# Routing split into eight planned steps with its temporaries in PSUM, a longer planned transpose, and a new table of order

## The chip, the core and the metric

The kernel runs on one core of one Trainium2 chip. The metric is device time in microseconds (us). The core has a matrix engine (PE), a vector engine (DVE), an activation engine (ACT), a general engine (POOL) and a queue engine that issues transfers (SP). Each takes its own instructions strictly in the order in which they were written, and engines wait for each other at semaphores.

## What is computed

Three stages in a row, on 1,536 tokens of 512 numbers: attention with a window of 128 and 4 sink positions, a dense layer of 2,048 hidden units with a rational activation, and a mixture of 8 experts in which each token goes to the expert of its largest logit and only as many tokens per expert as a capacity allows are kept.

```python
scores = scale * np.matmul(q, k.transpose(0, 1, 3, 2))
scores = np.where(is_sink | in_window, scores, -1000000000.0)
a = softmax(scores); x = np.matmul(a, v)
h = x @ w_in
g = (a[0] + a[1]*h + a[2]*h**2 + a[3]*h**3) / (1 + abs(b[0])*abs(h) + abs(b[1])*h**2 + 1e-6)
x = g @ w_out
logits = x @ w_gate
expert_idx = np.argmax(logits, axis=1)
gate_w = softmax(logits)[np.arange(N), expert_idx]
...
for i in range(N):          # in order of tokens
    e = expert_idx[i]
    if counts[e] < capacity:
        disp[e, counts[e]] = x[i]; pos[i] = counts[e]; counts[e] += 1; keep[i] = True
h = np.maximum(np.einsum('ecd,edf->ecf', disp, w1), 0.0)
y = np.einsum('ecf,efd->ecd', h, w2)
out[i] = gate_w[i] * y[expert_idx[i], pos[i]]       # for kept i
```

## The kernel before

All large products are made of half-precision pairs (a high and a low part), three matmuls for one. The work comes in these kinds.

- **Attention halves** (`half(n)`, 24 of them): scores (L649), mask, maximum and exponentials, transposes by PE (L707, L711), the product with v (L763, L765), and the split of the result into the tile `xt`.
- **Conversion of weights** (`conv`): each piece of w_in and w_out arrives as 64-bit numbers and is turned into a high and a low half. A letter per piece, in the strings CI and CO, says how: P and R use PE matmuls (L285 opens a bank, L279 subtracts), S and G finish on POOL (L335, L355), V finishes on DVE (L345). S and R keep a temporary `wf` in SBUF.
- **Units** (`unit(U)`, 24): four groups of 12 matmuls each (L827) of the dense layer for 256 tokens, then the rational function (`rat1` on ACT and DVE, `rat2` on POOL, `sig` on ACT), ended on DVE by L1433 from a bank or by L862 from SBUF, as the string RE says, and for the first two groups of tokens split into halves (`split`, L363 and then L366 on POOL or L369 on DVE, as the string GS says).
- **Gate columns** (`wg_group(f)`, 16): once piece f of w_out is converted, two transposing transfers (L877) bring it into a buffer `wf`, of which there are three, and 12 small matmuls (L885) multiply it with the gate's weights.
- **Bursts** (`burst`) add the units' shares of the logits; `logits` brings them to the layout by tokens (L971, L974).
- **Routing** of the first 512 tokens: `route` chooses the largest logit (`choose`, `first_max`: L955 to L981), counts the tokens per expert before each (`places`: L988, L990, the two matmuls L992 and L993, then L995 to L997) and works out the gate (`gates`, L1002 to L1006). `pick` then takes the expert with the most tokens (L1032 to L1051).
- **The chosen expert**: `ffn_y` multiplies the first 384 tokens with w_out (L1106) as soon as `pick` is through; the expert's own weights then take w_out's place; `hid` (L1126) and `outp` (L1150) follow. Remaining tokens' units go on meanwhile, and `count_rest` at the end says whether anything is left for a loop that isn't entered with these inputs.

The order of instructions on all engines is set before the program exists, by a planner (`Plan`). Each step is a generator that yields what it needs, an engine, a planned time and buffers, such as `yield DVE(1.9, "b")` for 1.9 us of DVE and a bank, and then writes its instructions. The planner takes the step that can start first on its engine, and among equal ones that with the smallest key. `DVL` is a DVE step that may not run beside POOL in the plan; `lat=` is added to the planned end of an SP step before a follower may start. Keys, and which engine does what, come from the table PRM. Where the plan leaves PE idle before 150 us and a bank is free, `idle` writes small filler matmuls (L490) that compute nothing, so that the matrix engine doesn't rest.

In `route`, all of `choose` and `places`, PE's two matmuls among them, are one step that is planned as 1.9 us of DVE:

```python
bs = slice(0, FB)
yield DVE(1.9, "b")
kb = plan.got("b")
mx = choose(bs)
places(bs, bank(kb))
plan.give("b", kb)
yield ACT(0.6)
gates(bs, mx)
```

So the two matmuls are written into PE's order at the point that PE's plan has reached by then, and take no planned time there.

Of the kernel before, what the change touches and what calls it, by code (L numbers as in the profile page):

```python
# [8 lines left out]
F32 = mybir.dt.float32  # L9
# [10 lines left out]
P = 128  # L20
# [8 lines left out]
E = 8  # L29
# [6 lines left out]
CH = 256  # L36
NCH = NT // CH
NU = 4 * NCH
PRM = dict(LA=11.877, RATE=1.2, LC=6.882, LO=2.195, BATCH=1, T0=-13.679, dS=1.29, TW=53.523, dW=7.072,
           T1=-22.973, d1=6.206, T2=67.305, d2=5.26, CI='PSPPSGGGGGGGVPPG', CO='GGGSVGPRVSSSSGPP',  # L40
           RE='PPPPSPPPPPSPPSSSPPPPPPSS', CC='G', LL=3, rb=5, gp=5, GS='GGGGGGGG', VE=1, rr=19.539, rs=36.318,
           rt=-29.499, LD=-6.009, TF=150, FG=0.033, NE=7, eps=0, WT=-60.39, NB=4, VS1=14, BK=-29.251, dK=12.297,
           dO=0.252, eb=2, SE='G', st=2, wf=3, rc=1, xt=2, ab=2, qb=2)


class Plan:
# [147 lines left out]
def SP(dur, *take, lat=0.0):  # L194
    return "SP", dur, take, lat, None, None
# [10 lines left out]
def _build(ctx, tc, nc, io, ns, window, cap):  # L206
# [36 lines left out]
    def bank(k):  # L243
        return (bps[0] if k < R["NB"] else bps[1]).tile([P, 512], F32, name=f"b{k}")
# [704 lines left out]
    keep = gat.tile([P, NBLK], F32, name="keep")  # L949
    run = gat.tile([P, NBLK + 1, E], F16, name="run")  # L950

    def first_max(dst, src, n):

        mx = sm.tile([P, NBLK], F32, name="fm")[:, :n]
        V.tensor_reduce(out=mx, in_=src, axis=AX.X, op=ALU.max)  # L955
        iv = sm.tile([P, NBLK, E], F32, name="fi")[:, :n]
        V.tensor_tensor(out=iv, in0=src, in1=mx.unsqueeze(2).to_broadcast([P, n, E]), op=ALU.is_ge)
        V.tensor_tensor(out=iv, in0=iv, in1=iom.unsqueeze(1).to_broadcast([P, n, E]), op=ALU.mult)
        ix = sm.tile([P, NBLK], F32, name="fx")[:, :n]
        V.tensor_reduce(out=ix, in_=iv, axis=AX.X, op=ALU.min)  # L960
# [13 lines left out]
        V.tensor_copy(out=lg[:, b0:b0 + nb, :], in_=lt[:, 0:nb * E].rearrange("p (t e) -> p t e", e=E))  # L974
        plan.give("b", kb)

    def choose(bs):

        n = bs.stop - bs.start
        mx, _ = first_max(oh[:, bs, :], lg[:, bs, :], n)  # L980
        V.tensor_copy(out=oh16[:, bs, :], in_=oh[:, bs, :])  # L981
        return mx

    def places(bs, pt):

        n = bs.stop - bs.start
# [34 lines left out]
    NSB = NST // P
# [6 lines left out]
    def pick():  # L1028
# [594 lines left out]
```

## Time and profile before

| | us |
|---|---|
| median of 3 runs (lowest, highest) | 341.65 (340.46, 343.74) |
| time of the profiled execution | 342.39 |
| its span, first instruction to last | 340.8 |
| PE busy, share of the span | 321.9, 94% |
| DVE busy | 258.8, 76% |
| ACT busy | 236.6, 69% |
| POOL busy | 199.7, 59% |
| mean granted clock of PE | 0.986 |

Busy time of PE counts the filler matmuls too. [...]

### The profile page before, as it was taken

To read this page: it belongs to the slowest core of one execution; us is meant where nothing else is said; L and a number is where in the kernel's file an instruction comes from. 1 tells how busy PE (TensorE), PEld (TensorE's weight loads), DVE (VectorE), ACT (ScalarE), POOL (GpSimd) and SP (SyncE) were. 2 spreads that over 40 slices of the span, in tenths; PEclk is the share of its full clock that TensorE was granted. 3 is DMA by queue.
4 is the path that set the end of the run, shared out by engine and by line. 5 is a ranking of instruction groups with operands and counts; after the bars stand their busy time and mean duration, and the time that the engine had idled before them with its cause. 6 is when DMAs were issued, how large, how long until landed. Compare 5 with 4: busy or idle time off the path is not lost.

```text
span 340.8 us, 9053 instructions
## 1 busy us (share of the span) xinstructions
PE 321.9 (94%) x3586; PEld 237.7 (70%) x3586; DVE 258.8 (76%) x505; ACT 236.6 (69%) x587; POOL 199.7 (59%) x211
## 2 busy tenths in 40 slices
PE   8999999989999889999999969999999999999991
PEld 5666787767878767878867748556676688787540
DVE  4988799899899898999898967502248689786541
ACT  2798989987989889897889746304255678686600
POOL 5466869759989587889998735305001156465400
PEclk9999999999999999999999969999999999999998
DMA  7655764727869998454861203000005320000011
GB/s 231 232 196 179 243 214 138 262 78 237 191 168 228 268 171 315 116 146 146 206 141 27 87 9 124 2 1 2 2 0 191 133 111 0 2 2 0 15 50 38
DMA packets 32744, 41.79 MB, mean 123 GB/s; under 512 B 19832, under 2 KB 19832, under 8 KB 32696
## 3 DMA queue, kind: packets, MB, share of 16 engines
q1 hardware_dynamic: 32696, 41.15, 41.6%
q8 instruction: 30, 0.49, 0.6%
q14 instruction: 18, 0.15, 0.2%
HBM read 30.66 MB, written 6.29 MB: 108 GB/s over the span
## 4 chain that ended last, share of the span: by engine, by line
PE 75%; DVE 14%; ACT 4%; DMA 3%; issue 2%; DVEq 0%; ACTq 0%
PE b L827 29%; PE b L1106 9%; PE b L490 7%; PE b L1150 5%; PE b L1126 5%; PE b L765 4%; PE sc L649 4%; PE b L707 3%; PE b L922 3%; DMA wf<-wout 2%; DVE b L315 2%; DVE g L1433 1%; PE b L279 1%; DMA st<-w_out 1%; PE b L763 1%
## 5 line engine op out<-in xcount | busy, mean ns | idle before, releaser
L827 PE MATMUL b<-xt,win 128*128 128x256 f16 x1152 | 139.6, 276 | 0.3
L827 PEld LDWEIGHTS <-win 128*128 128x128 f16 x1152 | 112.1, 100 | 21.1 <-issue 5.7
L852 POOL TENSOR_TENSOR rb<-rb,rc 128x1024 f32<-128x1024 f32 x24 | 57.5, 2396 | 1.4
L699 POOL TENSOR_TENSOR e<-e,rs 128x512 f32<-128x512 f32 x24 | 24.9, 1039 | 37.6 <-DVE rs L686 26.7
L831 ACT ACTIVATE rb<-b 128x512 f32<-128x512 f32 x48 | 28.9, 604 | 19.3 <-PE b L827 17.2
L835 DVE TENSOR_TENSOR g<-g,b 128x512 f32<-128x512 f32 x48 | 32.6, 681 | 10.8 <-ACT g L833 10.6
L849 POOL TENSOR_SCALAR rc<-rb,cof 128x1024 f32<-128x1024 f32 x24 | 28.9, 1202 | 20.0 <-ACT rb L831 19.7
L833 ACT ACTIVATE g<-b,cof 128x512 f32<-128x512 f32 x48 | 37.5, 784 | 0.0
L837 DVE SCALAR_TENSOR_TENSOR g<-g,cof,b 128x512 f32<-128x512 f32 x48 | 35.5, 742 | 0.7
L734 POOL TENSOR_SCALAR_AFFINE_SELECT upp<-low 128x512 f32<-128x512 f32 x20 | 13.4, 671 | 36.6 <-ACT low L728 36.5
L679 ACT ACTIVATE e<-sc,nm 128x132 f32<-128x132 f32 x84 | 31.3, 372 | 1.9
L1106 PE MATMUL b<-gs,wout 128*128 128x384 f16 x192 | 32.6, 326 | 0.0
L490 PE MATMUL b<-const-bfloat16-1.0 128*1 128x256 bf16 x201 | 29.5, 291 | 1.8 <-PEq L1612 0.9
L855 ACT ACTIVATE rb<-rb 128x1024 f32<-128x1024 f32 x24 | 25.6, 1065 | 3.7 <-POOL rb L852 3.7
L1106 PEld LDWEIGHTS <-wout 128*128 128x128 f16 x192 | 18.4, 99 | 13.2 <-issue 1.8
L490 PEld LDWEIGHTS <-const-bfloat16-1.0 128*1 128x1 bf16 x201 | 16.0, 88 | 12.4 <-issue 6.2
L1433 DVE SCALAR_TENSOR_TENSOR g<-g,cof,b 128x512 f32<-128x512 f32 x34 | 24.3, 742 | 0.5
L649 PE MATMUL sc<-kt,qt 64*64 64x128 f32 (+4 forms) x672 | 19.8, 249 | 1.9 <-DVE rs L682 1.9
L649 PEld LDWEIGHTS sc<-kt,qt 64*64 64x64 f32 x672 | 17.0, 132 | 6.0 <-issue 2.1
L1421 ACT ACTIVATE b<-rb 128x512 f32<-128x512 f32 x34 | 20.3, 611 | 0.5 <-DVE wgo L896 0.4
L366 POOL TENSOR_TENSOR gs<-g,gs 128x1024 f16<-128x1024 f32 (+1 forms) x8 | 13.2, 1649 | 10.5 <-ACT gs L363 10.5
L1108 ACT ACTIVATE gse<-b 128x384 f16<-128x384 f32 x4 | 2.0, 491 | 24.9 <-PE b L1106 24.9
(183 smaller groups left out, 626.8 us busy)
## 6 DMA issues: line engine op xcount, KB each, us to landing
st<-w_in SPq DMA_DIRECT2D x16, 512.0 KB, 4.1
st<-w_out SPq DMA_DIRECT2D x16, 512.0 KB, 3.9
st<-w SPq DMA_DIRECT2D x8, 512.0 KB, 3.3
kt<-k SPq DMA_DIRECT2D x12, 264.0 KB, 4.2
qt<-q SPq DMA_DIRECT2D x12, 256.0 KB, 3.6
v<-v SPq DMA_DIRECT2D x12, 256.0 KB, 2.9
xs<-xt SPq DMA_DIRECT2D x12, 256.0 KB, 3.3
out<-wf SPq DMA_DIRECT2D x12, 256.0 KB, 4.7
```

Source lines behind the costliest of these rows:

```text
L490: T.matmul(out=fp[0:1, 0:256], lhsT=one[:, 0:1], rhs=one, start=True, stop=True)
L649: T.matmul(out=out, lhsT=q[:, t], rhs=kk[:, a:z], start=True, stop=True)
L679: A.activation(out=e[:, h, :], in_=wv[:, h, :], func=AF.Exp, scale=0.125, bias=nm[:, h:h + 1], accum_out=su[:, h:h + 1])
L827: T.matmul(out=out, lhsT=l, rhs=r, start=(j == 0), stop=(j == len(jobs) - 1))
L831: A.activation(out=bb, in_=hp, func=AF.Abs, scale=2.0 ** -16)
L833: A.activation(out=g, in_=hp, func=AF.Identity, scale=cof[:, 3:4], bias=cof[:, 2:3])
L835: V.tensor_tensor(out=g, in0=g, in1=hp, op=ALU.mult)
L837: V.scalar_tensor_tensor(out=g, in0=g, scalar=cof[:, 1:2], in1=hp, op0=ALU.add, op1=ALU.mult)
L849: (G if eng == "G" else V).tensor_scalar(out=cc, in0=bb, scalar1=cof[:, 5:6], scalar2=cof[:, 4:5], op0=ALU.mult, op1=ALU.add)
L852: G.tensor_tensor(out=bb, in0=bb, in1=cc, op=ALU.mult)
L1106: T.matmul(out=yp[:, :n], lhsT=l, rhs=r, start=(j == 0), stop=(j == len(jobs) - 1))
L1433: V.scalar_tensor_tensor(out=g, in0=g, scalar=cof[:, 0:1], in1=rp[U, z], op0=ALU.add, op1=ALU.mult)
```

## The change

The step of the routing is cut into eight: choose (1.2 us of DVE planned), counts (0.8, DVL), places (0.2 of PE, now a PE step of its own), kept, gates_in, gates_exp, gates_out. The temporaries of `first_max`, `places`, `gates` and `pick`, tiles in SBUF before, lie in unused columns of the PSUM bank that the step holds anyway; `count_rest` takes a bank for it. What stays in SBUF are `lg`, `oh`, `oh16`, `run`, `keep`, `gw`. `pick` becomes two DVE steps and holds its bank longer. The transposes of `wg_group` are planned as 1.3 us with 2.2 us behind them (1.2 and 1.2 before). PRM gets other numbers throughout, and so every engine another order. Of the 24 units, 13 end by P instead of 17 (RE), two splits move from POOL to DVE (GS), and of the 32 pieces of weights (CI and CO together) 5 instead of 8 go by P, 3 instead of 1 by R, 3 instead of 7 by S, 16 instead of 13 by G and 5 instead of 3 by V.

```diff
-           T1=-22.973, d1=6.206, T2=67.305, d2=5.26, CI='PSPPSGGGGGGGVPPG', CO='GGGSVGPRVSSSSGPP',
-           RE='PPPPSPPPPPSPPSSSPPPPPPSS', CC='G', LL=3, rb=5, gp=5, GS='GGGGGGGG', VE=1, rr=19.539, rs=36.318,
+           T1=-23.716, d1=7.69, T2=79.004, d2=7.972, CI='PRGGGGGGGGGGRPPG', CO='GGVVVVPRVSSSGGGP',
+           RE='PPPPSPPPPPSPSPSSSSSPPSSS', CC='G', LL=3, rb=5, gp=5, GS='GGGGVVGG', VE=1, rr=50.47, rs=75.665,
...
-        yield SP(1.2, "wf", lat=1.2)
+        yield SP(1.3, "wf", lat=2.2)
...
-    def first_max(dst, src, n):
-
-        mx = sm.tile([P, NBLK], F32, name="fm")[:, :n]
+    def first_max(dst, src, n, pb):
+
+        mx, ix, iv = pb[:, 0:n], pb[:, 32:32 + n], in_bank(pb, n)
         V.tensor_reduce(out=mx, in_=src, axis=AX.X, op=ALU.max)
-        iv = sm.tile([P, NBLK, E], F32, name="fi")[:, :n]
...
+    def in_bank(pb, n):
+        return pb[:, 64:64 + n * E].rearrange("p (t e) -> p t e", e=E)
...
+    def counts(bs):
+
         if bs.start == 0:
             V.memset(run[:, 0, :], 0.0)
         for t in range(bs.start, bs.stop):
             V.tensor_tensor(out=run[:, t + 1, :], in0=run[:, t, :], in1=oh16[:, t, :], op=ALU.add)
...
     def route():
         bs = slice(0, FB)
-        yield DVE(1.9, "b")
+        yield DVE(1.2, "b")
         kb = plan.got("b")
-        mx = choose(bs)
-        places(bs, bank(kb))
+        pt = bank(kb)
+        pb = pt[:, NBLK * E:]
+        mx = choose(bs, pb)
+        yield DVL(0.8)
+        counts(bs)
+        yield PE(0.2)
+        places(bs, pt)
+        yield DVE(0.6)
+        kept(bs, pt, pb)
+        yield DVE(0.2)
+        gates_in(bs, mx, pb)
+        yield ACT(0.2)
+        gates_exp(bs, pb)
+        yield DVE(0.6)
+        gates_out(bs, pb)
         plan.give("b", kb)
-        yield ACT(0.6)
-        gates(bs, mx)
```

Three places of the new order. In these rows `b` with a number is a bank, `oh` the chosen expert of a token, `run` the counts, `wf` the buffer of the gate columns; line numbers are those of the version shown.

DVE at the routing, before:

```order
L974 COPY lg<-b_3609 128x32
L720 SCALAR_TENSOR_TENSOR sh_3593<-b_3591,sh_3593 32x128
L955 TENSOR_REDUCE fm<-lg 128x4
L957 TENSOR_TENSOR fi<-lg,fm 128x32
L958 TENSOR_TENSOR fi<-fi,iom 128x32
L960 TENSOR_REDUCE fx<-fi 128x4
L961 TENSOR_TENSOR oh<-fx,iom 128x32
L981 CAST oh_134<-oh 128x32
L988 MEMSET run 128x4
L990 TENSOR_TENSOR run<-run,oh_134 128x8 x4
L995 TENSOR_TENSOR po<-b_3649,oh 128x32
L996 TENSOR_REDUCE keep<-po 128x4
```

DVE at the routing, with the change:

```order
L972 COPY lg<-b_3646 128x32
L955 TENSOR_REDUCE b_3662<-lg 128x4
L956 TENSOR_TENSOR b_3662<-lg,b_3662 128x32
L957 TENSOR_TENSOR b_3662<-b_3662,iom 128x32
L958 TENSOR_REDUCE b_3662<-b_3662 128x4
L959 TENSOR_TENSOR oh<-b_3662,iom 128x32
L982 CAST oh_134<-oh 128x32
L835 TENSOR_TENSOR g_3532<-g_3532,b_3615 128x512
L988 MEMSET run 128x4
L990 TENSOR_TENSOR run<-run,oh_134 128x8 x4
L720 SCALAR_TENSOR_TENSOR sh_3659<-b_3657,sh_3659 32x128
L1465 SCALAR_TENSOR_TENSOR g_3265<-g_3265,cof,b_3712 128x512
```

The bank b_3662 stands where fm, fi and fx stood, and one step of a unit (L835) and a later pair of others now stand between the routing's own instructions; the first reader of the matmuls' result (L995 before) comes two rows below the end of this piece.

PE from the logits on, before, and the rows around the two matmuls of `places`:

```order
L971 MATMUL b_3609<-gsel,lacc_2592 128x8 x4
L279 LDWEIGHTS n_88
L279 MATMUL b_3572<-xt_3086,n_88 128x256
L827 LDWEIGHTS win_97
L827 MATMUL b_3622<-xt_2276,win_97 128x256
```

```order
L827 LDWEIGHTS win_98
L827 MATMUL b_3622<-xt_2276,win_98 128x256
L992 LDWEIGHTS tri_89
L992 MATMUL b_3649<-oh_134,tri_89 128x32
L993 LDWEIGHTS ones_86
L993 MATMUL b_3649<-run,ones_86 128x32
```

PE with the change, at the same two points:

```order
L969 MATMUL b_3646<-gsel,lacc_2445 128x8 x4
L707 MATMUL b_3652<-ident,e_3512 128x128 x4
L711 MATMUL b_3657<-ident,es_127 96x128
L649 MATMUL sc<-kt_2834,qt_3074 64x132
L649 MATMUL sc<-kt_3149,qt_3074 64x2x64
L649 MATMUL sc<-kt_3149,qt_3074 64x64
L649 MATMUL sc<-kt_2834,qt_3074 64x68
L649 MATMUL sc<-kt_2834,qt_3074 64x132
```

```order
L827 LDWEIGHTS win_98
L827 MATMUL b_3689<-xt_2309,win_98 128x256
L994 LDWEIGHTS tri_89
L994 MATMUL b_3662<-oh_134,tri_89 128x32
L995 LDWEIGHTS ones_86
L995 MATMUL b_3662<-run,ones_86 128x32
```

Between the logits' matmuls and those of `places` stand one subtraction and 12 matmuls of a unit before; with the change it is five transposes, 16 score matmuls and 24 matmuls of units.

SP at the first transposes, before:

```order
L295 DMA st_1595<-w_out 128x1024
L596 DMA v_1627<-v 128x512
L295 DMA st_1643<-w_out 128x1024
L877 DMA_TRANSPOSE wf_1701<-wout_99 128x4x128
L877 DMA_TRANSPOSE wf_1701<-wout_100 128x4x128
L295 DMA st_1728<-w_out 128x1024
L877 DMA_TRANSPOSE wf_1806<-wout_99 128x4x128
L877 DMA_TRANSPOSE wf_1806<-wout_100 128x4x128
L295 DMA st_1842<-w_out 128x1024
L877 DMA_TRANSPOSE wf_1876<-wout_99 128x4x128
L877 DMA_TRANSPOSE wf_1876<-wout_100 128x4x128
```

SP at the first transposes, with the change:

```order
L596 DMA v_1660<-v 128x512
L295 DMA st_1713<-w_out 128x1024
L877 DMA_TRANSPOSE wf_1742<-wout_99 128x4x128
L877 DMA_TRANSPOSE wf_1742<-wout_100 128x4x128
L877 DMA_TRANSPOSE wf_1765<-wout_99 128x4x128
L877 DMA_TRANSPOSE wf_1765<-wout_100 128x4x128
L877 DMA_TRANSPOSE wf_1797<-wout_99 128x4x128
L877 DMA_TRANSPOSE wf_1797<-wout_100 128x4x128
L295 DMA st_1833<-w_out 128x1024
```

Three pairs of transposes now follow each other with no other transfer between, where each pair had the load of a piece of w_out behind it.

Counted over the whole order, filler matmuls (L490) go from 201 to 164, L285 from 18 to 16 and L279 of 512 columns from 9 to 8; all other matmuls are the same in number. On DVE, the L369 of 512 elements go from 0 to 4, L345 from 3 to 5, L862 from 7 to 11, L1433 from 34 to 26; L325 into `wf` from 7 to 3. On POOL, L335 goes from 7 to 3, L355 from 20 to 19 and the splits of 512 elements (L366) from 8 to 4. Ahead of the logits of the first 512 tokens, PE has 720 matmuls of units where it had 672, and DVE 29 of L835 and of L837 where it had 28, and three L862 where it had two.

## Rows read from the trace of the kernel before

**Rows 1.** The page's first part: busy us of each engine, share, instructions

```profile
PE 321.9 (94%) x3586; PEld 237.7 (70%) x3586; DVE 258.8 (76%) x505; ACT 236.6 (69%) x587; POOL 199.7 (59%) x211
```

**Rows 2.** Sums by stretch: length, busy of each engine, clock, DMA share, GB/s

```profile
42.66:192.97 150.31, 144.15 (x1920) 114.67 (x1919) 139.35 (x261) 131.38 (x345) 123.23 (x114) 1.00 0.65 173
192.97:198.79 5.82, 2.70 (x27) 2.30 (x24) 4.90 (x15) 4.19 (x15) 4.71 (x4) 0.92 0.39 132
198.79:205.48 6.69, 6.69 (x37) 4.88 (x37) 2.83 (x12) 2.44 (x4) 1.26 (x2) 0.56 0.01 2
205.48:333.60 128.12, 128.12 (x1074) 87.70 (x1071) 77.29 (x136) 67.41 (x119) 44.09 (x30) 1.00 0.12 42
```

**Rows 3.** Timeline of PE around the routing: start, length, what, idle before it

```profile
193.99 1.47 PE L827 MATMUL b<-xt,win 128*128 128x256 f16 x12
198.15 0.19 PE L992 MATMUL b<-oh,tri 128*128 128x32 f16 x1 [2.69 <-DVE run L988]
198.77 0.19 PE L993 MATMUL b<-run,ones 128*128 128x32 f16 x1 [0.43 <-DVE run L990]
```

**Rows 4.** Timeline of DVE and POOL at the routing

```profile
194.06 0.19 DVE L974 COPY lg<-b 128x32 f32<-128x32 f32 x1 [0.54 <-PE b L971]
...
194.82 0.19 DVE L957 TENSOR_TENSOR fi<-lg,fm 128x32 f32<-128x32 f32 x1
...
195.05 0.53 DVE L958 TENSOR_TENSOR fi<-fi,iom 128x32 f32<-128x32 f32 x1
...
195.51 2.33 POOL L852 TENSOR_TENSOR rb<-rb,rc 128x1024 f32<-128x1024 f32 x1
...
195.83 2.06 DVE L961 TENSOR_TENSOR oh<-fx,iom 128x32 f32<-128x32 f32 x1
...
198.16 0.75 DVE L990 TENSOR_TENSOR run<-run,oh 128x8 f16<-128x8 f16 x4
...
198.99 0.19 DVE L995 TENSOR_TENSOR po<-b,oh 128x32 f32<-128x32 f32 x1
```

**Rows 5.** The chain that ended last: start, length, what

```profile
79.93 1.75 PE b L490 x15
...
114.52 3.93 PE b L827 x36
...
198.96 6.79 PE b L827 x36
...
208.65 2.64 PE b L827 x24
```

**Rows 6.** Groups by form: count, busy us, mean ns of one

```profile
L490 PE MATMUL b<-const-bfloat16-1.0 128*1 128x256 bf16 x201 | 29.5, 291 | 1.8 <-PEq L1612 0.9 <-ACT xt L785 0.8
L837 DVE SCALAR_TENSOR_TENSOR g<-g,cof,b 128x512 f32<-128x512 f32 x48 | 35.5, 742 | 0.7
L325 DVE SCALAR_TENSOR_TENSOR b<-st,b 128x512 int32<-128x512 int32 x24 | 16.6, 691 | 0.3
L325 DVE SCALAR_TENSOR_TENSOR wf<-st,wf 128x512 int32<-128x512 int32 x7 | 9.7, 1389 | 0.1
L862 DVE SCALAR_TENSOR_TENSOR g<-g,cof,rb 128x1024 f32<-128x1024 f32 x7 | 9.2, 1317 | 0.8 <-ACT rb L858 0.8
L345 DVE SCALAR_TENSOR_TENSOR wout<-b,wout 128x512 f16<-128x512 f32 x2 | 1.4, 688 | 0.0
L285 PE MATMUL b<-const-bfloat16-1.0 128*128 128x256 bf16 x18 | 3.5, 275 | 1.1 <-DVE g L1433 1.0
```

**Rows 7.** Line L369 alone: shortest, median and longest ns

```profile
L369 DVE SCALAR_TENSOR_TENSOR wout<-st,wout x8: 1210/1221/2887, 253.7 to 277.4; 128x1024 f16<-128x1024 f32 x8
```

**Rows 8.** The transposes: all landings of the tile, and timelines of SP and PE

```profile
DMA to landing us min/median/max: 2.4/4.0/6.7
...
118.88 5.20 SPq L877 DMA_TRANSPOSE wf<-wout x4
...
126.91 0.29 PE L885 MATMUL b<-wf,gate 128*32 128x128 f16 x8 [1.42 <-DMA wf<-wout]
```

More of the change, by code (lines that the diff above doesn't have):

```diff
@@ L38 @@
 NU = 4 * NCH
-PRM = dict(LA=11.877, RATE=1.2, LC=6.882, LO=2.195, BATCH=1, T0=-13.679, dS=1.29, TW=53.523, dW=7.072,
-           T1=-22.973, d1=6.206, T2=67.305, d2=5.26, CI='PSPPSGGGGGGGVPPG', CO='GGGSVGPRVSSSSGPP',
-           RE='PPPPSPPPPPSPPSSSPPPPPPSS', CC='G', LL=3, rb=5, gp=5, GS='GGGGGGGG', VE=1, rr=19.539, rs=36.318,
-           rt=-29.499, LD=-6.009, TF=150, FG=0.033, NE=7, eps=0, WT=-60.39, NB=4, VS1=14, BK=-29.251, dK=12.297,
-           dO=0.252, eb=2, SE='G', st=2, wf=3, rc=1, xt=2, ab=2, qb=2)
+PRM = dict(LA=11.665, RATE=1.2, LC=6.278, LO=2.398, BATCH=1, T0=-6.339, dS=1.466, TW=101.908, dW=8.497,
+           T1=-23.716, d1=7.69, T2=79.004, d2=7.972, CI='PRGGGGGGGGGGRPPG', CO='GGVVVVPRVSSSGGGP',
+           RE='PPPPSPPPPPSPSPSSSSSPPSSS', CC='G', LL=3, rb=5, gp=5, GS='GGGGVVGG', VE=1, rr=50.47, rs=75.665,
+           rt=-23.946, LD=-5.978, TF=150, FG=0.033, NE=7, eps=0, WT=-55.976, NB=4, VS1=14, BK=-48.295,
+           dK=18.198, dO=0.133, eb=2, SE='G', st=2, wf=3, rc=1, xt=2, ab=2, qb=2)
 class Plan:
@@ L975, in logits, with choose @@
         plan.give("b", kb)
-    def choose(bs):
+    def in_bank(pb, n):
+        return pb[:, 64:64 + n * E].rearrange("p (t e) -> p t e", e=E)
+    def choose(bs, pb):
         n = bs.stop - bs.start
-        mx, _ = first_max(oh[:, bs, :], lg[:, bs, :], n)
+        mx, _ = first_max(oh[:, bs, :], lg[:, bs, :], n, pb)
         V.tensor_copy(out=oh16[:, bs, :], in_=oh[:, bs, :])
         return mx
-    def places(bs, pt):
-        n = bs.stop - bs.start
+    def counts(bs):
         if bs.start == 0:
@@ L990, in places, with kept @@
             V.tensor_tensor(out=run[:, t + 1, :], in0=run[:, t, :], in1=oh16[:, t, :], op=ALU.add)
-        pv = pt[:, 0:n * E]
+    def places(bs, pt):
+        pv = pt[:, 0:(bs.stop - bs.start) * E]
         T.matmul(out=pv, lhsT=tri16, rhs=oh16[:, bs, :].rearrange("p t e -> p (t e)"), start=True, stop=False)
         T.matmul(out=pv, lhsT=ones16, rhs=run[:, bs, :].rearrange("p t e -> p (t e)"), start=False, stop=True)
-        ov = sm.tile([P, NBLK, E], F32, name="po")[:, :n]
+    def kept(bs, pt, pb):
+        n = bs.stop - bs.start
+        pv = pt[:, 0:n * E]
+        ov = in_bank(pb, n)
         V.tensor_tensor(out=ov, in0=pv.rearrange("p (t e) -> p t e", e=E), in1=oh[:, bs, :], op=ALU.mult)
@@ L997, in places, with gates_in, gates_exp, gates_out @@
         V.tensor_scalar(out=keep[:, bs], in0=keep[:, bs], scalar1=float(cap), scalar2=None, op0=ALU.is_lt)
-    def gates(bs, mx):
+    def gates_in(bs, mx, pb):
         n = bs.stop - bs.start
-        ex = sm.tile([P, NBLK, E], F32, name="ex")[:, :n]
+        ex = in_bank(pb, n)
         V.tensor_tensor(out=ex, in0=lg[:, bs, :], in1=mx.unsqueeze(2).to_broadcast([P, n, E]), op=ALU.subtract)
+    def gates_exp(bs, pb):
+        ex = in_bank(pb, bs.stop - bs.start)
         A.activation(out=ex, in_=ex, func=AF.Exp)
+    def gates_out(bs, pb):
+        ex = in_bank(pb, bs.stop - bs.start)
         V.tensor_reduce(out=gw[:, bs], in_=ex, axis=AX.X, op=ALU.add)
@@ L1032, in pick @@
         T.matmul(out=cp[:, 0:E], lhsT=ones16, rhs=run[:, NSB, :], start=True, stop=True)
-        yield DVE(1.9)
+        yield DVE(1.3)
         cn = sm.tile([P, E], F32, name="cn")
         V.tensor_copy(out=cn, in_=cp[:, 0:E])
-        plan.give("b", kb)
-        _, ix = first_max(e0oh.unsqueeze(1), cn.unsqueeze(1), 1)
+        pb = cp[:, NBLK * E:]
+        _, ix = first_max(e0oh.unsqueeze(1), cn.unsqueeze(1), 1, pb)
         V.tensor_scalar(out=e0i, in0=ix, scalar1=float(E), scalar2=None, op0=ALU.add)
-        t = sm.tile([P, NSB, E], F32, name="stt")
+        yield DVE(0.8)
+        t = in_bank(pb, NSB)
         V.tensor_tensor(out=t, in0=oh[:, 0:NSB, :], in1=e0oh.unsqueeze(1).to_broadcast([P, NSB, E]), op=ALU.mult)
@@ L1044, in pick @@
         V.tensor_copy(out=s16, in_=stm)
+        plan.give("b", kb)
         yield PE(0.05, "b")
@@ L1173, in count_rest @@
         bs = slice(FB, NBLK)
-        yield DVE(1.2)
-        choose(bs)
+        yield DVE(1.5, "b")
+        kb = plan.got("b")
+        choose(bs, bank(kb))
+        plan.give("b", kb)
         ct = sm.tile([P, E], F32, name="cn")
@@ L1191, in rest_blocks @@
         bs = slice(FB, NBLK)
-        mx = choose(bs)
-        places(bs, bank(0))
-        gates(bs, mx)
+        pt, pb = bank(0), bank(1)
+        mx = choose(bs, pb)
+        counts(bs)
+        places(bs, pt)
+        kept(bs, pt, pb)
+        gates_in(bs, mx, pb)
+        gates_exp(bs, pb)
+        gates_out(bs, pb)
         V.tensor_copy(out=rest, in_=keep)
```

1 line of the change is left out of this document (removed).

## The prediction

> **What bounds the kernel now.** I read the page's busy times first: PE is busy for 321.9 of the span of 340.8 us, so the time is PE's work plus the time in which PE waits or idles [rows 1]. But 201 of its matmuls are filler, 29.5 us of that busy time [rows 6]; they do nothing but occupy idle time that the plan foresaw. So at most some 48 us (29.5 of filler and 18.9 of idle) can be won by order alone. The sums by stretch then show three regimes [rows 2]. From the first unit at 42.66 to the logits at 192.97, PE is busy for 144.2 of 150.3 us and DVE for 139.4, that is 93%: both are close to full. From 205.48 to 333.6 PE has no idle time at all (128.12 of 128.12) and DVE is at 60%: there PE alone sets the time. In between lies the routing, 192.97 to 205.48, where PE stands still first and then runs slowly.
>
> The timelines show why. PE meets the two matmuls of the places right after 12 matmuls of a unit, waits 2.69 us for DVE's counts, and 0.43 more for the last of them [rows 3]. DVE was working on the routing all that time: from the copy of the logits at 194.06 to the fourth count at 198.91 it needs 4.85 us, 2.06 of which is one instruction, L961, on 32 elements per partition, where L957 on as many takes 0.19 [rows 4]. It ends at 197.89; POOL's L852, which began before it, ends at 197.84. L958 shows the same on a small scale (0.53). So two instructions with both inputs in SBUF stood in a queue behind POOL, for 1.87 and 0.34 us. [...]
>
> **The change, part by part.** The sum is made against the profiled execution: span 340.8, time 342.39, so 1.6 lie outside the span, and the median of the runs is 0.74 below that execution.
>
> *Routing.* The places become a PE step that the plan puts where DVE is done. In the new order 24 matmuls of units stand ahead of them (2.64 us by the chain's row of the same number [rows 5]), with five transposes and 16 score matmuls before those, against one subtraction and 12 matmuls (1.47) now. DVE needs for the same stretch seven small instructions and four counts, 11 at 0.19 by L957, L974 and L990 [rows 4], and an L835 that now lies among them, 0.7 at most by L837 [rows 6]: 2.8 us, if none queues behind POOL. The cover is above 2.64 by the transposes and scores, so the wait goes: 2.69 + 0.43 = -3.1. With it goes the slow stretch, 6.79 - 3.93 = -2.9. Together -6.0. Bounds: 0, if DVE comes as late as now; nothing beyond -6.0.
>
> The PSUM temporaries themselves I cost at nothing: L995, which reads a bank, takes 0.19 like L957, which reads SBUF [rows 4]. [...]
>
> *Filler.* 37 fewer L490. The ones in question are in the middle of the program; there 15 take 1.75 us [rows 5], 0.117 each: -4.3. By the mean of all (29.5 / 201 [rows 6]), which contains the slow first ones, it would be -5.4. The other bound is 0: if PE must wait there anyway, leaving the filler out shortens nothing. I take -4.3, since in the trace PE runs from filler straight into work. The two L285 fewer (3.5 / 18, 0.2 each [rows 6]) and one L279 fewer make -0.6.
>
> *DVE ahead of the logits.* This is the cost. Up to the copy of the logits DVE gets one more L835 and L837 (1.4), one more L862 (1.3), two more L345 (1.4) [rows 6] and four L369 of half size, 0.6 each by half of the median of 1221 ns [rows 7], 2.4; half a us of small ones; and four fewer L325 into `wf`, which take 1389 ns where those into a bank take 691 [rows 6], so -2.8. Sum +4.2. Of it about 2.7, the units' part, is work taken over from after the routing, where DVE has time. PE's own work ahead of the logits stays as it is: 48 more matmuls of units (at 3.93 / 36, +5.2) for the filler and the three others that go (-4.9). What is 5.2 more before the logits is 5.2 less after them, in the stretch where PE is the only limit. So if PE sets the pace before the routing too, DVE's +4.2 costs nothing, hidden by DVE's own idle time of 11 us in that stretch; if DVE sets it, nearly all of it shows. Both are close to full, and I take the middle: +2, bounds 0 and +4.2. An L369 can be held up to 2.9 us [rows 7], which is why the upper bound isn't lower.
>
> *Transposes.* Sixteen pairs. A pair takes SP 2.6 us to issue (5.20 for two), a landing takes 2.4 to 6.7 us, and once PE waits 1.42 for it [rows 8]. Planning one more us between issue and use moves the 12 matmuls behind other work; that can win the 1.42. Against it, three pairs now stand in a row on SP, so the third is issued at least 5.2 us after the first began, while PE has its 12 matmuls only five transposes and one other matmul behind the second's. I take 0, bounds -1.4 and +5.
>
> *Behind the routing.* PE's work is the same pieces in another order; the last unit has 52 matmuls of the output between it and its burst, as now, and the last transfer comes after the last matmuls as now. 0.
>
> Sum: -6.0 - 4.3 - 0.6 + 2 + 0 = -8.9. Span 340.8 - 8.9 = 331.9; time 331.9 + 1.6 = 333.5 for a profiled execution, less 0.74 for the median: **332.8**.
>
> **The rivals.**
>
> *DVE sets the pace before the routing.* Then the logits come 4.2 later instead of as now, whatever filler is left out, and 5.2 less follows behind them: 340.8 - 6.0 + 4.2 - 5.2 = 333.8 of span, 334.7 as a median. For it: 93% on DVE, the fullest that any stretch shows [rows 2]. Against it: POOL loses four L366 and four L335, so DVE queues less behind it. With a late DVE the routing's wait is likelier too.
>
> *The routing's wait stays.* The counts are still sums of two tiles in SBUF; if an L852 (2.33 [rows 4]) runs when the first of them is due, DVE needs 2.8 + 2.3 = 5.1 us. For it: L961's row. Against it: in the trace none of the four counts was held (0.75 for four [rows 4]). With a wait and the slow clock as before, 332.8 + 6.0 = 338.8, and 334.7 + 6.0 = 340.7 where DVE sets the pace as well. [...]
>
> *Transposes stop PE.* This one ends slower. With three pairs in a row PE stands before the third set for up to 2.6 + 2.6 us of issue less little, 5.0 at the most, and a wait as long as the routing's would take the clock with it, as there, 2.9 more: 8 us. At one place it gives 341, no change. It needs two such places to be slower, 332.8 + 16 = 348.8, and decides from PE waiting there at both for longer than it now does at the routing's matmuls. Against it: the one wait that the trace shows is 1.42, and two pairs in a row caused it.
>
> **How the numbers follow.** The forecast and what lies near it has 0.58; DVE's pace 0.14, the routing's wait 0.18, the transposes at two places 0.07, some other new wait with the slow clock 0.03. One per cent, 3.4 us, is about what a measurement of this kernel tells from no change: 338.2 and 345.1. Faster: 0.58 + 0.14, and 0.05 of the routing's wait where DVE costs nothing beside it: 0.77. Same: 0.13 + 0.03 = 0.16. Slower: 0.07. Low end: -6.0 - 5.4 - 0.6 + 0 - 1.4 = -13.4, so 328.3, and I go to 327.5 for waits that another order may lose; high end 340.7, the routing's wait with DVE's pace.
>
> **What would show it.** Right: no wait above 0.5 us before the places' matmuls, the instructions of the choice at 0.2 us each whatever POOL does, a granted clock of 1.00 from the first units to the end, the first L1106 only about one us earlier than now, since 36 more matmuls of units lie ahead of it by the order, and 164 L490 of about 25 us. Wrong on DVE: PE's idle time between 42 and 193 us above the 6.2 of now, most of it ended by DVE. Wrong on the transposes: PE before L885 waiting for the transfers for more than 3 us. The prediction fails altogether if a new wait as long as the routing's appears elsewhere and the granted clock falls behind it.

## The result, and the profile after

The changed kernel takes 335.73 us (median of 4 runs, 335.24 to 339.25) against 341.92 for the kernel before beside it on the same chip: a ratio of 0.984, 95% interval 0.980 to 0.988. By the ratio that is 1.6%, some 5.4 us; the two medians lie 6.2 us apart. The profiled execution took 335.6, its span is 334.0 and the mean granted clock 0.998. Ratios and ranges here and below are of fast executions alone; slower ones, such as one of the kernel before at 371.8 us and a clock of 0.846, are left out. In the fences below line numbers are those of the kernel shown.

The page's busy times, which answer to [rows 1], and its shares of the chain by engine:

```profile
PE 312.9 (94%) x3546; PEld 232.3 (70%) x3546; DVE 264.6 (79%) x507; ACT 235.5 (71%) x585; POOL 191.9 (57%) x202
...
PE 58%; DVE 27%; DMA 7%; ACT 4%; issue 2%; SPq 0%; DVEq 0%
```

Before, the chain ran 75% over PE and 14% over DVE. So the part of the chain that lies on DVE is now nearly twice as long.

PE in the timeline around the routing, against [rows 3] (start, length, what, idle before it):

```profile
196.10 0.96 PE L969 MATMUL b<-gsel,lacc 128*128 128x8 f32 x8
201.10 0.18 PE L994 MATMUL b<-oh,tri 128*128 128x32 f16 x1
201.13 0.18 PE L995 MATMUL b<-run,ones 128*128 128x32 f16 x1
```

DVE and POOL there, against [rows 4]:

```profile
194.13 2.36 POOL L852 TENSOR_TENSOR rb<-rb,rc 128x1024 f32<-128x1024 f32 x1
...
197.09 0.19 DVE L972 COPY lg<-b 128x32 f32<-128x32 f32 x1 [1.08 <-PE b L969]
...
197.78 0.20 DVE L957 TENSOR_TENSOR b<-b,iom 128x32 f32<-128x32 f32 x1
...
198.47 0.18 DVE L982 CAST oh<-oh 128x32 f16<-128x32 f32 x1
...
199.29 1.35 DVE L990 TENSOR_TENSOR run<-run,oh 128x8 f16<-128x8 f16 x4
...
201.72 2.36 POOL L852 TENSOR_TENSOR rb<-rb,rc 128x1024 f32<-128x1024 f32 x1
...
202.76 1.34 DVE L1003 TENSOR_SCALAR keep<-keep 128x4 f32<-128x4 f32 x1
```

The two matmuls of the places wait for nothing. Every instruction of the choice takes 0.2 us; but note the first row: POOL's L852 had ended at 196.49, before the choice began. The next L852 does lie across the routing, and the one instruction there that reads and writes SBUF alone, the test of `keep`, is held by it until 204.1 (1.34 us).

The counts took 1.35 us, and not 0.75 as before. Cut to single instructions, the timeline shows why:

```profile
199.07 0.64 POOL L734 TENSOR_SCALAR_AFFINE_SELECT upp<-low 128x512 f32<-128x512 f32 x1 [2.59 <-ACT low L728]
199.29 0.43 DVE L990 TENSOR_TENSOR run<-run,oh 128x8 f16<-128x8 f16 x1
...
199.78 0.65 POOL L737 TENSOR_SCALAR_AFFINE_SELECT low<-low 128x512 f32<-128x512 f32 x1
...
199.95 0.48 DVE L990 TENSOR_TENSOR run<-run,oh 128x8 f16<-128x8 f16 x1
```

The first and the third count, which take 0.16 us when nothing holds them, ended within 0.02 us of POOL's L734 and L737. So the counts did queue behind POOL, though not behind an L852.

Sums by stretch, of before and of after, cut at the first unit, the logits' matmuls, the first matmul of `ffn_y` and PE's last one (columns as in [rows 2]). The first unit of the kernel before starts at 37.00; the 42.66 of the prediction is a later one. First before, all of PE's work and then the filler L490 alone:

```profile
0.00:37.00 37.00, 34.74 (x458) 23.35 (x459) 29.12 (x72) 25.38 (x88) 21.33 (x54) 1.00 0.62 205
37.00:192.97 155.97, 149.62 (x2002) 119.47 (x1999) 143.82 (x270) 136.71 (x362) 128.25 (x122) 1.00 0.66 177
192.97:211.49 18.52, 15.40 (x142) 12.61 (x139) 13.00 (x44) 10.97 (x28) 9.38 (x10) 0.82 0.24 77
211.49:333.60 122.11, 122.11 (x994) 82.28 (x993) 72.02 (x119) 63.07 (x111) 40.68 (x27) 1.00 0.11 39
...
0.00:37.00 37.00, 19.84 (x131) 11.01 (x131) 1.00 0.62 205
37.00:192.97 155.97, 9.68 (x70) 5.03 (x70) 1.00 0.66 177
```

and after, in the same way:

```profile
0.00:35.70 35.70, 30.66 (x432) 21.38 (x433) 28.91 (x73) 26.37 (x93) 21.30 (x54) 1.00 0.65 212
35.70:196.10 160.40, 152.52 (x2034) 122.92 (x2033) 147.13 (x282) 140.41 (x374) 125.63 (x120) 1.00 0.66 178
196.10:212.09 15.99, 14.73 (x201) 12.37 (x200) 14.08 (x47) 11.60 (x27) 7.29 (x8) 1.00 0.09 22
212.09:327.50 115.41, 114.91 (x884) 75.66 (x883) 74.02 (x106) 56.67 (x91) 37.64 (x24) 1.00 0.14 44
...
0.00:35.70 35.70, 15.32 (x109) 9.48 (x109) 1.00 0.65 212
35.70:196.10 160.40, 7.86 (x55) 3.78 (x55) 1.00 0.66 178
```

The span's 6.8 us come from the stretches so: -1.3 up to the first unit, +4.4 to the logits, -2.5 to `ffn_y`, -6.7 to PE's last matmul, -0.7 behind it (7.2 to 6.5). By kind of time it reads more plainly. PE's work without filler goes from 292.4 to 289.6 us (-2.7): 1.9 of it lie in the units' matmuls (139.6 to 137.7), some of which ran at the clock of 0.82 in the third stretch, now 1.00, and 0.8 in the two L285 and the one L279 that are fewer. Filler goes from 29.5 to 23.2 (-6.3). PE's idle time goes from 11.7 to 14.7, although 3.12 of the 11.7, the two waits before the places, are gone: everywhere else it grew by 6.1. With the 0.7 at the end: -2.7 - 3.1 - 6.3 + 6.1 - 0.7 = -6.7, the 6.8 but for rounding. **What the missing filler gave, other idle time took back.**

PE's longest waits after (us in total, times, longest); 5.4 of these rows are waits for DVE:

```profile
PE b L279 <- ACT xt L780: 2.4, 5, 0.8
PE b L490 <- DVE g L837: 1.9, 1, 1.9
PE b L763 <- DVE g L1465: 1.7, 1, 1.7
PE b L763 <- DVE wout L345: 1.1, 1, 1.1
...
PE b L827 <- DVE g L1465: 0.7, 2, 0.5
...
PE b L885 <- DMA wf<-wout: 0.5, 2, 0.3
```

Groups by form, against [rows 6]:

```profile
L490 PE MATMUL b<-const-bfloat16-1.0 128*1 128x256 bf16 x164 | 23.2, 289 | 3.9 <-DVE g L837 1.9 <-ACT low L728 1.1 <-PEq L1644 0.9
L862 DVE SCALAR_TENSOR_TENSOR g<-g,cof,rb 128x1024 f32<-128x1024 f32 x11 | 19.1, 1738 | 2.6 <-ACT rb L858 2.6
```

L862, which has two inputs and its output in SBUF, takes 1738 ns on average where it took 1317. The prediction had counted the one more ahead of the logits at 1.3 us.

### The profile page after: what moved, and what is told of

It is laid out like the page before. It is cut to its first block, busy times and chain, and to the rows that moved or that the text cites. A ratio compares the mean times of both kernels' runs of the same rounds, so it can differ in the third digit from the quotient of the medians.

```text
span 334.0 us, 8969 instructions
## 1 busy us (share of the span) xinstructions
PE 312.9 (94%) x3546; PEld 232.3 (70%) x3546; DVE 264.6 (79%) x507; ACT 235.5 (71%) x585; POOL 191.9 (57%) x202
## 4 chain that ended last, share of the span: by engine, by line
PE 58%; DVE 27%; DMA 7%; ACT 4%; issue 2%; SPq 0%; DVEq 0%
PE b L827 19%; PE b L1131 9%; DMA st<-w_out 5%; PE b L1175 5%; PE b L490 4%; PE b L1151 4%; PE sc L649 3%; PE b L765 3%; DVE g L1465 3%; DVE g L837 3%; DVE g L835 3%; PE b L922 2%; PE b L707 2%; DVE b L315 2%; DVE sc L657 2%
## 5 line engine op out<-in xcount | busy, mean ns | idle before, releaser
L827 PE MATMUL b<-xt,win 128*128 128x256 f16 x1152 | 137.7, 273 | 1.3 <-DVE g L1465 0.7
L827 PEld LDWEIGHTS <-win 128*128 128x128 f16 x1152 | 110.2, 98 | 20.9 <-issue 5.7
L849 POOL TENSOR_SCALAR rc<-rb,cof 128x1024 f32<-128x1024 f32 x24 | 29.9, 1248 | 56.9 <-ACT rb L831 49.1
L852 POOL TENSOR_TENSOR rb<-rb,rc 128x1024 f32<-128x1024 f32 x24 | 58.9, 2455 | 1.3
L835 DVE TENSOR_TENSOR g<-g,b 128x512 f32<-128x512 f32 x48 | 32.4, 678 | 10.9 <-ACT g L833 10.8
L699 POOL TENSOR_TENSOR e<-e,rs 128x512 f32<-128x512 f32 x24 | 25.5, 1061 | 23.7 <-DVE rs L686 7.7
L837 DVE SCALAR_TENSOR_TENSOR g<-g,cof,b 128x512 f32<-128x512 f32 x48 | 35.5, 739 | 0.5
L490 PE MATMUL b<-const-bfloat16-1.0 128*1 128x256 bf16 x164 | 23.2, 289 | 3.9 <-DVE g L837 1.9
L315 DVE TENSOR_SCALAR b<-st 128x512 int32<-128x512 int32 x26 | 17.9, 688 | 5.8 <-DMA st<-w_out 4.1
L734 POOL TENSOR_SCALAR_AFFINE_SELECT upp<-low 128x512 f32<-128x512 f32 x20 | 13.4, 672 | 14.5 <-ACT low L728 14.4
L490 PEld LDWEIGHTS <-const-bfloat16-1.0 128*1 128x1 bf16 x164 | 13.3, 88 | 12.0 <-issue 7.2
L862 DVE SCALAR_TENSOR_TENSOR g<-g,cof,rb 128x1024 f32<-128x1024 f32 x11 | 19.1, 1738 | 2.6 <-ACT rb L858 2.6
L329 DVE SCALAR_TENSOR_TENSOR b<-st,b 128x512 int32<-128x512 int32 x29 | 20.0, 689 | 0.2
L1465 DVE SCALAR_TENSOR_TENSOR g<-g,cof,b 128x512 f32<-128x512 f32 x26 | 18.9, 738 | 0.8 <-ACT b L1453 0.7
```

Of the source, the lines that this page charges most:

```text
L490: T.matmul(out=fp[0:1, 0:256], lhsT=one[:, 0:1], rhs=one, start=True, stop=True)
L827: T.matmul(out=out, lhsT=l, rhs=r, start=(j == 0), stop=(j == len(jobs) - 1))
L835: V.tensor_tensor(out=g, in0=g, in1=hp, op=ALU.mult)
L837: V.scalar_tensor_tensor(out=g, in0=g, scalar=cof[:, 1:2], in1=hp, op0=ALU.add, op1=ALU.mult)
L849: (G if eng == "G" else V).tensor_scalar(out=cc, in0=bb, scalar1=cof[:, 5:6], scalar2=cof[:, 4:5], op0=ALU.mult, op1=ALU.add)
L852: G.tensor_tensor(out=bb, in0=bb, in1=cc, op=ALU.mult)
```

## The experiments

Each ratio is against the kernel before on the same chip; microseconds are worked out as (ratio - 1) x 342, unless medians are named.

| run | median us | ratio (95% interval) |
|---|---|---|
| e1: steps and PSUM, old table | 338.6 | 0.994 (0.991 to 0.997) |
| e2: new table, old routing | 336.2 | 0.984 (0.980 to 0.988) |
| e3: the change, temporaries in SBUF | 334.1 | 0.979 (0.975 to 0.983) |
| e4: before, temporaries of the choice in PSUM | 341.0 | 1.001 (0.997 to 1.004) |
| e5: before, choice, cast and counts through the bank | 338.3 | 0.992 (0.990 to 0.995) |
| e6: the change, cast, counts and `keep` through the bank | 333.3 | 0.978 (0.975 to 0.981) |
| e7: the change itself again | 335.3 | 0.985 (0.981 to 0.989) |
| e8: before, longer transposes | 347.2 | 1.020 (1.016 to 1.023) |
| e9: before, no filler after 40 us | 339.1 | 0.993 (0.990 to 0.997) |
| e10: the change, no filler after 40 us | 335.4 | 0.982 (0.975 to 0.988) |
| e11: before, eight more DVE copies | 346.9 | 1.016 (1.010 to 1.022) |
| e12: the change, eight more DVE copies | 340.2 | 0.996 (0.993 to 0.999) |

**The parts apart: e1, e2, e8.** e1 is the changed kernel with the old table and the old numbers of the transposes, e2 the kernel before with the new ones, e8 the kernel before with this line alone:

```diff
-        yield SP(1.2, "wf", lat=1.2)
+        yield SP(1.3, "wf", lat=2.2)
```

> The eight steps and the PSUM temporaries, with the table and the transposes' planned times of before. Theory 1 (the steps are worth the routing's wait and the slow clock behind it, 3.1 + 2.9, and the new table nothing, because the filler that it saves comes back as waits for DVE): 341.9 - 6.0 = 335.9 us, no wait above 0.5 us before the places' matmuls, granted clock 1.00 there. Theory 2 (table and steps share the gain about evenly): 338.5 to 339.5 us.

> The new table and the longer transposes, with the routing as one step and its temporaries in SBUF as before. Only four transposes and one more stand between the logits and the places' matmuls here, so PE must wait for DVE's 2.1 to 5 us there. Theory 1: 340 to 343 us, a wait of 2.5 to 4.5 us at the places and a lower granted clock behind it. Theory 2 (the table alone is worth 3 us): 337 to 339 us even with that wait.

> The kernel before with the transposes planned as 1.3 and 2.2 behind them, and nothing else. 198 fillers by its order, 768 matmuls of units ahead of the logits, and only five transposes and a subtraction between these and the places' matmuls. If the longer plan is what gains: 337 to 339 us, with no wait of PE for a transfer before L885. If it merely moves the order: 340 to 342 us, with the routing's wait as large as before or larger.

The steps alone give 2.2 us, the table with the transposes' numbers 5.4, both together 5.4 as well (5.1 in e7): the parts don't add, and the theory that the steps bring the whole of the gain and the table nothing falls. The table alone brings as much as the whole change, more than either theory had for e2; what the steps add on top of it, these runs can't tell from nothing. In e2 the places still wait, but only 1.02 + 0.42 us, since POOL's L852 has ended before the choice; the granted clock is 1.00 from 192.97 to 211.49 us, across that wait, where before it was 0.82:

```profile
196.22 2.36 POOL L852 TENSOR_TENSOR rb<-rb,rc 128x1024 f32<-128x1024 f32 x1
...
200.31 0.19 DVE L961 TENSOR_TENSOR oh<-fx,iom 128x32 f32<-128x32 f32 x1
...
200.77 0.19 PE L992 MATMUL b<-oh,tri 128*128 128x32 f16 x1 [1.02 <-DVE run L988]
```

So L961, the 2.06 us of before [rows 4], costs 0.19 with nothing done to it but another order. e1 shows the opposite: with the old table L852 lay across the choice (195.80 to 198.15) and the cast of `oh` took 2.15. The places' first matmul waits for nothing there, as theory 1 had it, but the second does, since another instruction of POOL held a count:

```profile
199.85 1.57 DVE L990 TENSOR_TENSOR run<-run,oh 128x8 f16<-128x8 f16 x4
199.94 1.04 POOL L699 TENSOR_TENSOR e<-e,rs 128x512 f32<-128x512 f32 x1 [1.78 <-DVE run L988]
...
201.27 0.18 PE L995 MATMUL b<-run,ones 128*128 128x32 f16 x1 [1.57 <-DVE run L990]
```

With the transposes' numbers alone the planner makes an order that is 2.0% slower, which neither expectation had; PE waits nowhere for `wf` there, it waits for DVE at other places, the longest being:

```profile
PE b L1088 <- DVE wg L902: 1.6, 1, 1.6
PE sc L649 <- DVE rs L682: 1.6, 2, 1.3
```

A planned time is thus no cost of its own; it moves everything else.

**The temporaries and POOL: e3, e4, e5, e6.** e3 takes the changed kernel's order and puts the temporaries back into SBUF; e4 takes the kernel before and moves the choice's temporaries into its bank; e5 and e6 besides take the cast and the counts out of SBUF, so that up to the places no routing instruction has SBUF on all sides except, in e5, the first reduction (L955). From e5:

```diff
-        V.tensor_copy(out=oh16[:, bs, :], in_=oh[:, bs, :])
+        V.tensor_tensor(out=oh16[:, bs, :], in0=ix.unsqueeze(2).to_broadcast([P, n, E]),
+                        in1=iom.unsqueeze(1).to_broadcast([P, n, E]), op=ALU.is_equal)
...
-            V.memset(run[:, 0, :], 0.0)
-        for t in range(bs.start, bs.stop):
-            V.tensor_tensor(out=run[:, t + 1, :], in0=run[:, t, :], in1=oh16[:, t, :], op=ALU.add)
+            rp = pb[:, 64:64 + (n + 1) * E].rearrange("p (t e) -> p t e", e=E)
+            V.memset(rp[:, 0, :], 0.0)
+            for t in range(n):
+                V.tensor_tensor(out=rp[:, t + 1, :], in0=rp[:, t, :], in1=oh16[:, t, :], op=ALU.add)
+            V.tensor_copy(out=run[:, 0:n + 1, :], in_=rp)
```

> The changed kernel in the same order of instructions, with the temporaries of the routing back in SBUF. If the steps do it and the place of the temporaries is a detail: DVE's two instructions can queue behind POOL for up to 2.2 us, 2.8 + 2.2 = 5.0 against a cover of some 4.2, so at most 0.8 more: 335.7 to 336.5 us. If PSUM is what does it: the wait comes back with the slow clock, 340 to 342 us.

> The kernel before in the same order of instructions, with the two temporaries on which DVE queued behind POOL (the index list and its minimum) in the PSUM bank. If the place alone is enough: DVE needs 4.85 - 2.2 = 2.65 us against a cover of 1.7, PE waits about 0.9 us, the clock stays at 1.00: 341.9 - 2.2 - 2.9 = 336.8 us. If the wait of 0.9 is still followed by the lower clock: 339.7 us. If only the steps help: 341 to 342 us.

> The kernel before in its order, with no instruction of the choice and the counts that both reads and writes SBUF alone: the half-precision copy of the choice is computed a second time from the bank, the counts are summed in the bank and copied out once. Theory 3 (the routing's price is one instruction, whichever comes first, that queues behind POOL, and the clock that falls behind PE's wait): DVE needs 14 instructions of 0.19 and one of 0.28, 2.9 us, against a cover of 1.7; PE waits about 1.2 us instead of 3.1 and the clock stays at 1.00: 340.9 - 1.9 - 2.9 = 336.1 us. If the clock falls behind 1.2 us too: 339. Rival (the gain lies in the table alone, the routing's wait would be found elsewhere): 340 to 342 us.

> The changed kernel with the same removal, and the test on the capacity read from the bank as well. In the trace of the changed kernel the four counts took 1.35 instead of 0.75 and that test 1.34 instead of 0.17. Theory 3: up to 1.3 us less than the changed kernel of the same job, with no wait behind the test. Rival: the same within 0.5 us, since what DVE gains there it waits for elsewhere.

e3 is at least as fast as the change (334.1, below both expected ranges), so in the new order the bank is not what helps; its instructions of the choice take 0.19 us each in SBUF, where those that read a bank take 0.20 in the change. e4 shows where the queue goes when only a part of the instructions leave SBUF:

```profile
195.23 2.33 POOL L852 TENSOR_TENSOR rb<-rb,rc 128x1024 f32<-128x1024 f32 x1
195.24 0.19 DVE L965 TENSOR_TENSOR oh<-b,iom 128x32 f32<-128x32 f32 x1
195.47 2.13 DVE L985 CAST oh<-oh 128x32 f16<-128x32 f32 x1
...
197.65 0.18 PE L996 MATMUL b<-oh,tri 128*128 128x32 f16 x1 [2.47 <-DVE run L992]
```

The choice itself no longer waits, the cast right behind it does, until L852 ends, and PE waits 2.47 + 0.44 instead of 2.69 + 0.43; the ratio is 1.001. In e5 the same L852 lies across what replaces the cast and across the counts, and it holds none of them; PE still waits 1.61 us, about half of before:

```profile
196.23 2.34 POOL L852 TENSOR_TENSOR rb<-rb,rc 128x1024 f32<-128x1024 f32 x1
...
196.35 0.18 DVE L985 TENSOR_TENSOR oh<-b,iom 128x32 f16<-128x32 f32 x1
...
196.70 0.80 DVE L996 TENSOR_TENSOR b<-b,oh 128x8 f32<-128x8 f32 x4
...
197.79 0.18 PE L1002 MATMUL b<-oh,tri 128*128 128x32 f16 x1 [1.61 <-DVE run L997]
```

That gives 2.6 us with the order of before and the routing still in one step. The granted clock is 1.00 from 192.97 to 211.49 us, across that wait, where e4 shows 0.91 across its longer one. e6, the same edit on the changed kernel with the test of `keep` from the bank too (0.16 us across an L852, 1.34 in the change), has the lowest median of all, 333.3, 2.0 below e7 where 1.3 at most was expected; its interval just meets that of the change.

**The same kernel again: e7.**

> The changed kernel as it is, for the same chip as the other runs of this job: 335 to 336 us, ratio 0.984.

335.3, ratio 0.985: differences of under half a per cent between these runs mean nothing.

**Filler and DVE: e9 to e12.** The order is left as it is. e9 (before) and e10 (after) leave out the filler behind 40 us of the plan; e11 and e12 add eight copies on DVE between 100 and 190 us that nobody reads.

```diff
-                T.matmul(out=fp[0:1, 0:256], lhsT=one[:, 0:1], rhs=one, start=True, stop=True)
+                if t0 < 40.0:
+                    T.matmul(out=fp[0:1, 0:256], lhsT=one[:, 0:1], rhs=one, start=True, stop=True)
```

```diff
         V.scalar_tensor_tensor(out=g, in0=g, scalar=cof[:, 1:2], in1=hp, op0=ALU.add, op1=ALU.mult)
+        loads.append(0)
+        if 14 < len(loads) <= 22:
+            V.tensor_copy(out=extra, in_=hp)
```

> The kernel before, order unchanged, but without the 70 filler matmuls that the plan puts in after 40 us (201 to 131); they occupy about 70 x 0.117 = 8.2 us of PE. Theory 'filler stands in the way': PE runs on where it stood, the time falls by most of the 8.2, to 333 to 336. Theory 'PE must wait there anyway' (for DVE, ACT or a transfer): the idle time grows by what the filler gives up and the time stays within 1.5 of before, 340 to 342.5. Rival: the longer rests take the clock down at one or two places, 3.4 us each, and the kernel gets slower, 344 to 348.

> The changed kernel, order unchanged, without the 55 filler matmuls after 40 us (164 to 109), about 55 x 0.117 = 6.4 us of PE. Filler in the way: 335.7 - 5 = 330 to 332. PE waits there anyway: 334.5 to 336.5, with idle time of PE 5 to 6 us above the 21.1 of the changed kernel. Clock falls in the rests: 338 or more.

> The kernel before with eight more instructions on DVE between 100 and 190 us that nobody reads: a copy of a bank of 128x512 into a spare tile behind eight of the L837, unplanned, so the order of the rest is the same; about 8 x 0.69 = 5.5 us of DVE by L345's row. If DVE sets the pace there already: +4.5 to +5.5, 346 to 347. If PE and DVE share the pace, as the prediction's middle had it: +2.6, about 344. If PE sets it: within 1.5 of before.

> The changed kernel with the same eight instructions. Theory 'with the change DVE sets the pace ahead of the routing': +4.5 to +5.5, 340 to 341.5, and more than the same load costs the kernel before. Rival 'the new waits for DVE are places of the order, DVE has room elsewhere': +0 to +2.5, at most 338.2.

Without its 55 middle fillers the change takes 335.4, the same as with them (335.7, 335.3): PE has to wait there anyway. Without its 70 the kernel before gains 2.4 us (1.1 to 3.6) of the some 8.2 that they occupy. That lies between the two theories: in the kernel before a part of the filler did stand in the way, and the logits come 2.4 earlier there (at 190.56). The granted clock makes the size hard to read: it fell to 0.84 in the stretch where 4.0 us less of PE's time are filled (18.52 us busy there before), so a part of the gain may have been lost again (the expectation had 3.4 us for such a fall; at the routing of the kernel before the clock was 0.50 for 6.8 us, which is 3.4 at full speed):

```profile
60.00:80.00 20.00, 14.55 (x157) 10.85 (x156) 19.20 (x36) 18.57 (x47) 13.98 (x14) 0.84 0.56 186
...
190.56 1.06 PE L972 MATMUL b<-gsel,lacc 128*128 128x8 f32 x8
```

The copies on DVE answer the other question. In e11 they take 5.5 us, and the logits come later by 5.25 (198.22 instead of 192.97):

```profile
L842 DVE CAST extra<-b 128x512 f16<-128x512 f32 x8 | 5.5, 685 | 0.0
```

```profile
198.22 1.06 PE L976 MATMUL b<-gsel,lacc 128*128 128x8 f32 x8
...
203.41 0.18 PE L997 MATMUL b<-oh,tri 128*128 128x32 f16 x1 [2.70 <-DVE run L993]
```

The kernel before pays 5.5 us (3.4 to 7.5) for 5.5 us on DVE. The change pays 3.7 in span (334.0 to 337.7), some 4.0 by the ratios. The theory that DVE sets the pace only with the change falls: **more work on DVE shows in both kernels**, nearly whole in the one before, although PE's busy share of the stretch is the higher one. DVE isn't alone in it before, since e9 shows that less filler on PE wins something there too. The opposite load, more work on PE, was not tried.

## Why the prediction was right, and where it was not

Forecast 332.8, measured 335.7, within the range and faster as forecast, but by less: 8.85 us from the median before were forecast, 6.2 came by the medians and 5.4 by the ratio. By its own steps:

- **Routing, -6.0: nearly right in size, and half right in its reason.** The wait of 3.1 and the slow clock are gone together; the clock was put at -2.9, from the 36 matmuls of units that took 6.79 us behind the wait and 3.93 elsewhere [rows 5] (the granted clock of the kernel before was 0.50 from 197.9 to 204.7), and the units' matmuls take 1.9 less over the whole program. The price of the clock is that of the profiled execution: beside the experiments the kernel before took 338.3 to 340.5 us where its mean clock was 0.992 or more, and 341.3 to 343.5 at 0.985 or less. The 24 matmuls, five transposes and 16 score matmuls were cover enough, though DVE took 3.55 us from the logits' copy to the last count (197.09 to 200.64) and not 2.8, for POOL's L734 and L737 held two of the counts. The prediction had judged from one trace that none would be held; in e1 it costs a wait of 1.57. "Whatever POOL does" isn't shown either: POOL's L852 was over before the choice. The steps alone bring 2.2 (e1), the table without them 5.4 (e2), and the banks nothing (e3, e4); it is the order that takes L852 out of the way, or, in e5, the absence of instructions that POOL holds.
- **PSUM temporaries at nothing: right.** The instructions of the choice take 0.20 us where they read the bank (the change) and 0.19 with the temporaries in SBUF (e3), a difference of 0.01.
- **Filler, -4.3: the step that failed, in two ways.** It took the 37 for filler of the middle; 22 of them (131 to 109) stood ahead of the first unit, where 4.5 us less of filler let the units start only 1.3 us earlier. The 15 in the middle are 1.8 us. And the sentence that PE runs from filler straight into work was read as if the work could have come earlier. For the most part it could not: with the middle filler out, the change gains nothing (e10) and the kernel before 2.4 of 8.2 (e9). Its other bound, 0, was nearer than -4.3.
- **DVE ahead of the logits, +2: too little, by e11 and e12.** DVE's busy time from the first unit to the logits grew by 3.3 and the stretch by 4.4; e11 shows the logits 5.25 later for 5.5 more on DVE, e12 4.05 (at 200.15). The sign that the prediction named against itself appeared: PE's idle time between 42.66 us and the logits went from 6.2 to 7.9. The first rival, DVE's pace, had this mechanism, and gives a span of 333.8 where 334.0 was measured. That it comes so close is in part luck: it had the logits 4.2 later and 11.2 less behind them, and measured were 3.1 and 9.9. The better reading of "both close to full" would have been to count PE's filler as idle: 144.2 - 8.2 of PE's 150.3 us are work, 90%, and DVE's 139.4 are all work, 93% [rows 2].
- **L285 and L279, -0.6**: 16 and 8 of them as forecast; PE's busy time for these two kinds falls by 0.8, and what of it shows in the time can't be told apart.
- **Transposes, 0: right within its bounds.** PE's wait for `wf` goes from 1.4 to 0.5. The rival with two long waits there fell, and e8, where the numbers alone make an order that is slower, has none either.
- **Behind the routing, 0: nearly right.** PE's pieces of work are the same; 5.2 us more of them stand ahead of the logits now, as forecast, and 7.2 more ahead of `ffn_y`. The end of the program behind PE's last matmul is 0.7 shorter. The first matmul of `ffn_y` comes 0.6 later, where the text had it one earlier, for the reasons of the two terms above.

Filler and DVE together were forecast at -2.3 and measured at about -0.2 with the new waits (2.1 too much), the routing brought about 1.0 less than forecast by this count, and the end of the program gave 0.7 that no term had, L285 and L279 0.2 more than theirs: but for rounding the 2.1 us by which the span was missed. The median was missed by 2.9, also because the profiled execution lies 0.1 below it this time and not 0.74 above. What stays open is which half of the table, the letters of conversions and units or the keys, brings its 5.4 us, and where e6 gains over the change outside `keep`; neither was tried apart. Which of DVE's new pieces of work (L862, L345, L369) PE's new waits hang on was not tried either.

## What to carry to other kernels

An engine that shows 96% busy may be waiting all the same, if some of its work is filler: subtract what computes nothing before you ask who sets the pace, and test it by loading the other engine with work that nobody reads. Moving one temporary to another memory can move a queue behind another engine only to the next instruction that still works in the first alone (e4: from L961, 2.06 us before, to the cast, 2.13); take out all those that are held, or place the long instruction elsewhere. A change of a planner's table is one change of everything: cost a new order by the stretches that it makes, and not by the instructions that it saves.

## What the runs showed of the hardware that was not expected

- Instructions with one input queued behind POOL as well: the cast of `oh` from SBUF to SBUF took 2.13 (e4) and 2.15 us (e1) instead of 0.18, and the test of `keep`, on four elements per partition, 1.34 (the change) instead of 0.17. Each ended within 0.04 us of POOL's L852. The prediction had named only instructions with two inputs in SBUF.
- The counts, two SBUF inputs on eight elements, were held like that by POOL's shorter instructions too: in the change one took 0.43 and one 0.48 us until L734 and L737 ended, instead of 0.16, and in e1 the four took 1.57 across an L699, instead of 0.75. From a bank four took 0.80 across an L852 (e5).
- Not everything with SBUF on all sides was held. In e3 the reduction that makes `keep` reads and writes SBUF, and it took 0.19 us in the middle of an L852, which held the test right behind it for 1.35:

```profile
200.41 2.35 POOL L852 TENSOR_TENSOR rb<-rb,rc 128x1024 f32<-128x1024 f32 x1
...
201.22 0.19 DVE L1003 TENSOR_REDUCE keep<-po 128x4 f32<-128x32 f32 x1
```

- Where filler was left out, the granted clock fell in the middle of the program: to 0.84 in the stretch of e9 shown above, and in e10 the mean clock of the profiled execution was 0.986, 0.012 below the change. That went with longer times: the three executions of e10 at 0.986 or less took 335.8 to 337.1 us, the three at 0.993 or more 333.6 to 335.0. So at the higher clock leaving the filler out may be worth up to about one of its 6.4 us.
